# Attention, SoLU block and GELU-like block: the bias table from one position row with scalars, one layer-norm step deferred, products three chunks behind

## The chip, the cores and the metric

The kernel runs on one core of a Trainium2 chip. The metric is the time that the device needs for one execution, in microseconds (us). The engines are TensorE (PE in the profile; PEld is its weight load), VectorE (DVE), ScalarE (ACT), GpSimd (POOL) and SyncE (SP, which here only issues DMAs). Less is better.

## The reference

Three parts follow one another: attention with a position bias, a SoLU block with a layer norm, and a block with a piecewise quadratic activation. All is in float32.

```
scores = q @ k.T / sqrt(64)                     # 4 batches, 8 heads, 576 positions, 64 per head
x[i,j] = log1p(|i-j|) / log1p(max(i,1))
bias   = relu(x * w1 + b1) @ w2                 # 32 hidden values -> one bias for each head, i, j
attn   = softmax(scores + bias);  y = attn @ v  # y as 2304 rows of 512

h  = y @ w_in                                   # 512 -> 1024
s  = h * softmax(h)
ln = (s - mean(s)) / sqrt(var(s) + 1e-6) * g
z  = ln @ w_out                                 # 1024 -> 512

h2 = z @ w_in2                                  # 512 -> 2048
g2 = h2 if h2 >= 1; 0 if h2 <= -1; else (h2+1)^2/4
out = g2 @ w_out2                               # 2048 -> 512
```

In row i, x[i,j] depends on j only by log1p(|i-j|). Row 1 has log1p(distance) divided by log1p(1), which is log 2; every row i > 1 is row 1 times the reciprocal of its own entry at distance i.

## The kernel before

**Bias stage.** The table of all biases is written to DRAM (`bias_d`) before the attention starts, by 36 units of 16 rows i each. A unit u covers `span(u)` distances, between 304 and 576 (`n`, mean 440). A loaded constant holds x for all rows as a high and a low part (`xcon`, 18 loads, one for two units). `emit_z` (L226) spreads it: for each of four quarters c TensorE multiplies the rows (`xs`) by a selection table that holds w1 (`sel`), so that partition 32a + h holds x times w1[h] for one row; the results lie in PSUM as `z` (L235, and L240 for the columns past 512). `relu` (L220) adds b1 and takes the positive part, on ScalarE (L222) for the first pair of quarters and for the rest past 512, on VectorE (L224) for the second pair. `emit_c` (L245) multiplies these 128 x n tiles `r` by w2 on TensorE (L254), one quarter for each 32 output partitions, into `o`; ScalarE and VectorE copy `o` mirrored (L260) and straight (L264) to `ow`, and SyncE stores it (L269). The order on every engine is the order in which the code emits: `emit_z` of unit p, then `emit_c` of unit p - 1. `ow` has six buffers, `r` three. In between, `prep_all` (L172) prepares the first heads in steps of its generator: it casts q and k on VectorE to high parts (L181, L184) and subtracts on GpSimd for the low parts (L183, L186); one step is taken in every second unit. Loads of the stored table (`load_bias`) are issued after units 12, 17, 27, 33 and at the end, on SyncE's queue between the stores.

**Attention.** 144 chunks k (16 units of two heads, nine chunks each) run in an order that strings of letters write out: Q scores (L394) and their sum with the bias tile (L400), E exponential, T transposition, P product with v, B a step of `prep_all`, W a step of a conversion of the weights. B is left out in the first unit.

**SoLU and layer norm.** For each of 18 tiles of 128 rows: `emit_h` (L535), then `emit_post` (L541) as a generator: maximum (L553), exponential, product and sum (L558), square (L563), the inverse root on GpSimd (L568), and the last step: a multiplication of two columns on VectorE (L570) and the normalisation on ScalarE (L571). `emit_lt` transposes the tile two iterations later (L677, L681, L685), `emit_o` (L696) multiplies by w_out, and ScalarE copies the result out (L701). Steps of the conversion of the next weights (`bw`, L291 to L310 and L281) stand in between.

**Last block.** 80 chunks (j, f): `emit_h2` (L820) into `h`, then the activation to `ga` (L826 to L828), its high part `gh` on ScalarE (L829) and low part `gl` on VectorE (L831); `emit_o2` (L844) multiplies the chunk of two steps before by w_out2 and sums over f. `gh` and `gl` have three buffers.

## Time and profile before

| | us |
|---|---|
| median of three runs | 988.68 (986.91 to 991.41) |
| profiled execution | 988.0 |
| its span | 986.2 |
| TensorE busy | 966.6 (98%) |
| VectorE busy | 616.2 (62%) |
| ScalarE busy | 548.6 (56%) |
| GpSimd busy | 311.4 (32%) |

The span runs from the first to the last instruction of the profile; the profiled execution's own time lies 1.8 us above it. Matmuls are pipelined and their ends are modelled, so a busy TensorE is not one at its peak, but a gap in its row is real waiting. The granted TensorE clock is a share of full speed.

### The profile page before, as it was taken

Reading aid. Unit: us, or ns where it says so; the run is one execution under the profiler, and the core shown is the slowest. Engines: PE = TensorE matmul, PEld = TensorE weight load, DVE = VectorE, ACT = ScalarE, POOL = GpSimd, SP = SyncE. Lnnn points to the kernel's source line nnn. Section 1 sums busy time; section 2 is a strip of 40 time slices with the busy share of each in tenths; the row PEclk is TensorE's granted clock in tenths of the full one; section 3 lists DMA queues with packets and bytes.
Section 4 is the critical chain, followed back from the end, with each engine's and each line's share of the span. In section 5 each row is a group of like instructions: output and inputs, shape, how many; then the busy total and the mean of one; then the engine's idle time right before and its main releaser. Section 6 shows DMA issues by size and latency. Waiting matters only on the chain.

```text
span 986.2 us, 16218 instructions
## 1 busy us (share of the span) xinstructions
PE 966.6 (98%) x6112; PEld 798.4 (81%) x6112; DVE 616.2 (62%) x1232; ACT 548.6 (56%) x1116; POOL 311.4 (32%) x277
## 2 busy tenths in 40 slices
PE   9999999999999999999999899989999999999998
PEld 6447888888888878899998888768888888888897
DVE  6778878779779536777777747774434343433343
ACT  6888888889889856666666433332222222222232
POOL 3323455555555312555555423430010011000000
PEclk9999999999999999999999999999999999999999
DMA  6995474463562100234544468501000100100010
GB/s 188 281 302 166 140 235 138 137 221 127 175 198 100 36 15 8 86 129 150 171 160 160 160 241 304 200 14 64 12 11 1 64 21 1 53 7 6 1 43 22
DMA packets 50046, 112.21 MB, mean 114 GB/s; under 512 B 7600, under 2 KB 13872, under 8 KB 49968
## 3 DMA queue, kind: packets, MB, share of 16 engines
q1 hardware_dynamic: 42688, 101.72, 31.4%
q0 software_dynamic: 2384, 4.74, 1.8%
q10 hardware_dynamic: 4896, 4.72, 1.4%
q8 instruction: 48, 0.79, 0.3%
q14 instruction: 30, 0.25, 0.1%
HBM read 80.34 MB, written 30.82 MB: 113 GB/s over the span
## 4 chain that ended last, share of the span: by engine, by line
PE 40%; issue 8%; POOL 6%; DVE 5%; ACT 2%; DMA 0%; POOLq 0%; ACTq 0%; DVEq 0%
PE acc L844 17%; PE h L820 17%; PE ps_x L696 3%; PE ps_s L535 2%; POOL wp L304 2%; POOL wdl L281 2%; DVE ga L827 1%; POOL xl L519 1%; DVE wp L291 1%; DVE raw L294 1%; POOL stb L568 1%; DVE ga L828 1%; PE ps_s L696 1%; DVE wp L295 1%; ACT gh L829 1%
## 5 line engine op out<-in xcount | busy, mean ns | idle before, releaser
L827 DVE SCALAR_TENSOR_TENSOR ga<-ga 128x512 f32<-128x512 f32 (+1 forms) x80 | 56.8, 710 | 157.5 <-ACT ga L826 157.5
L826 ACT ACTIVATE ga<-h,half_c 128x512 f32<-128x512 f32 (+1 forms) x80 | 51.5, 644 | 131.1 <-PE h L820 131.1
L400 DVE CUSTOM_DVE_ANT_0 e<-ps_s,bt 128x576 f32<-128x576 f32 x144 | 106.6, 752 | 25.3 <-PE ps_s L394 22.2
L820 PE MATMUL h<-x2h,w2l 128*128 128x512 f32 (+1 forms) x320 | 117.7, 368 | 0.0
L820 PE MATMUL h<-x2l,w2h 128*128 128x512 f32 (+1 forms) x320 | 117.7, 368 | 0.0
L820 PE MATMUL h<-x2h,w2h 128*128 128x512 f32 (+1 forms) x320 | 117.6, 368 | 0.0
L415 ACT ACTIVATE e<-e,su 128x576 f32<-128x576 f32 x144 | 112.3, 781 | 6.5 <-DVE su L400 6.2
L844 PE MATMUL acc<-w2h,gh 128*128 128x512 f32 x288 | 112.7, 391 | 2.5 <-ACT gh L829 2.5
L304 POOL TENSOR_TENSOR wp<-raw,wp 128x256 f32<-128x256 f32 (+1 forms) x64 | 68.3, 1067 | 148.1 <-DVE wp L301 115.3
L844 PE MATMUL acc<-w2h,gl 128*128 128x512 f32 x288 | 112.5, 391 | 1.5 <-DVE gl L831 1.5
L829 ACT CAST gh<-ga 128x512 fp32r<-128x512 f32 (+1 forms) x80 | 46.2, 578 | 120.6 <-DVE ga L828 120.6
L844 PE MATMUL acc<-w2l,gh 128*128 128x512 f32 x288 | 112.3, 390 | 0.0
L733 POOL TENSOR_TENSOR x2l<-x2f,x2h 128x512 fp32r<-128x512 f32 (+1 forms) x20 | 25.6, 1281 | 253.2 <-ACT x2h L732 253.2
L394 PE MATMUL ps_s<-kh,sq 128*128 128x288 f32 x320 | 101.3, 334 | 3.7 <-DVE su L400 3.5
L458 ACT COPY pt<-ps_t 128x512 f32<-128x512 f32 x144 | 83.6, 581 | 24.1 <-PE ps_t L457 23.7
L394 PE MATMUL ps_s<-kl,sq 128*128 128x288 f32 x320 | 89.0, 294 | 0.0
L457 PE MATMUL ps_t<-ident,e 128*128 128x128 f32 x576 | 86.8, 274 | 0.0
L831 DVE TENSOR_TENSOR gl<-ga,gh 128x512 fp32r<-128x512 f32 (+1 forms) x80 | 52.3, 653 | 48.3 <-ACT gh L829 48.1
L696 PE MATMUL ps_x<-lh,woh 128*128 128x256 f32 x256 | 73.5, 287 | 6.4 <-ACT os L701 5.5
L457 PEld LDWEIGHTS ps_t<-ident,e 128*128 128x128 f32 x576 | 69.6, 141 | 5.7 <-ACT pt L458 2.1
L696 PE MATMUL ps_x<-ll,woh 128*128 128x256 f32 x256 | 72.1, 282 | 0.5 <-DVE ll L685 0.5
L696 PE MATMUL ps_x<-lh,wol 128*128 128x256 f32 x256 | 72.1, 281 | 0.0
(147 smaller groups left out, 2277.9 us busy)
## 6 DMA issues: line engine op xcount, KB each, us to landing
stg<-in_qk_dram SPq DMA_DIRECT2D x30, 640.0 KB, 3.9
raw<-in_w2nd_dram SPq DMA_DIRECT2D x32, 512.0 KB, 3.7
bias_d<-ow SPq DMA_DIRECT2D x36, 295.5 KB, 4.1
w_d<-wdh SPq DMA_DIRECT2D x20, 256.0 KB, 2.9
w_d<-wdl SPq DMA_DIRECT2D x20, 256.0 KB, 2.5
w2h<-w_d SPq DMA_DIRECT2D x10, 512.0 KB, 5.9
w2l<-w_d SPq DMA_DIRECT2D x10, 512.0 KB, 6.4
v<-in_vp_dram SPq DMA_DIRECT2D x15, 320.0 KB, 3.9
```

What stands on the lines that cost most here:

```text
L304: nc.gpsimd.tensor_tensor(out=p, in0=t, in1=p, op=ALU.mult)
L394: nc.tensor.matmul(sc[:, hf, 0:HS], lhsT=l, rhs=r, start=j == 0, stop=j == len(parts) - 1)
L400: nc.vector.tensor_tensor_reduce(out=halves(e), in0=sc[:, :, 0:HS], in1=halves(b_t[hp, n]), scale=-1.0 / float(D) ** 0.5, scalar=3.0e38, o ...
L415: nc.scalar.activation(out=e, in_=e, func=ACTF.Exp, scale=-1.0, bias=su[:, n:n + 1], accum_out=su[:, 9 + n:10 + n])
L457: nc.tensor.transpose(tp[:, kt * 128:(kt + 1) * 128], e[:, c0:c0 + 128], ident)
L458: nc.scalar.copy(out=pt[:, 4 * h:4 * h + 4, 128 * o:128 * o + 128], in_=tp.rearrange("p (a b) -> p a b", a=4))
L696: nc.tensor.matmul(ob[:, a * 256:(a + 1) * 256], lhsT=l, rhs=r[:, f, :], start=f == 0 and j == 0, stop=f == K1 - 1 and j == 2,)
L820: nc.tensor.matmul(hp_, lhsT=l, rhs=r[:, kk, 0:n], start=kk == 0 and q == 0, stop=kk == KD - 1 and q == 2)
L827: nc.vector.scalar_tensor_tensor(out=a, in0=a, scalar=1.0, in1=a, op0=ALU.min, op1=ALU.mult)
L829: nc.scalar.copy(out=gh[:, 0:n], in_=a)
L831: nc.vector.tensor_tensor(out=gl[:, 0:n], in0=a, in1=gh[:, 0:n].bitcast(F32), op=ALU.subtract)
L844: nc.tensor.matmul(acc_t[j][q], lhsT=l, rhs=r, start=f == 0 and m == 0, stop=f == K2 - 1 and m == 2)
```

## The change

The bias stage no longer loads `xcon` and multiplies it by a selection table. Only the row of position 1 is loaded, its high and its low part as the two partitions of `x1`; two products with ones add the parts and spread the sum to all 128 partitions, and ScalarE copies it to `xr`. VectorE takes the reciprocals of its elements, four quarters of the partitions each with its own stride, and multiplies them by w1 (`dg`), which gives one scalar for each partition and quarter (`sc1`). A quarter of r is then one instruction from SBUF to SBUF: on ScalarE relu(scale * xr + b1), on VectorE max(scale * xr, -b1), in which b1 is left out and its product with w2 is added at the end (`kc`). ScalarE takes the first quarter in four of five units. The copies of `o` to `ow` are two per unit, both on ScalarE, with the constant as bias. Of `prep_all` eight steps run in the bias stage, with the subtractions of the first unit on VectorE, and the first attention unit takes steps too. In the layer norm, the multiplication of the last step moves from VectorE to ScalarE, and the step is taken in the next iteration, behind the maximum and exponential of the next tile. In the last block the second product follows three chunks behind (two in the first five), with four buffers of `gh` and `gl`.

```
-    def load_x(rb): ... nc.gpsimd.dma_start(out=t[:, 0:n], in_=xcon[:, rb, 0:n])
+    nc.scalar.dma_start(out=x1, in_=bass.AP(xcon.tensor, xcon.offset + XR, [[32 * XR, 2], [1, S]]))
...
     for _ in range(8):
+        nc.tensor.matmul(wz[:, 0:128], lhsT=wt, rhs=wt, start=True, stop=True)
...
+    for hf in range(2):
+        nc.tensor.matmul(
+            zx[:, hf, 0:HS], lhsT=one2, rhs=x1[:, hf * HS:hf * HS + HS], start=True, stop=True
+        )
+    for _ in range(12):
+        nc.tensor.matmul(wz[:, 0:128], lhsT=wt, rhs=wt, start=True, stop=True)
+    nc.scalar.copy(out=halves(xr), in_=zx[:, :, 0:HS])
...
+    for a in range(4):
+        ps_ = slice(32 * a, 32 * a + 32)
+        rows = xr.rearrange("p (t a) -> p t a", a=4)[ps_, (1 if a == 0 else 0):S // 4, a]
+        nc.vector.reciprocal(out=sc1[ps_, (1 if a == 0 else 0):S // 4], in_=rows)
+    nc.vector.tensor_scalar(out=sc1, in0=sc1, scalar1=dg[:, 32:33], scalar2=None, op0=ALU.mult)
+    for c in range(4):
+        nc.tensor.matmul(z[32 * c:32 * c + 32, 256:258], lhsT=flat(w2b),
+            rhs=kc[:, 4:6] if c == 0 else b1c.to_broadcast([128, 2]), start=True, stop=True)
+    nc.vector.tensor_copy(kc[:, 1:3], z[:, 256:258])
...
-            nc.gpsimd.tensor_tensor(out=kl, in0=ks, in1=kh.bitcast(F32), op=ALU.subtract)
+            eng = nc.vector if u == 0 else nc.gpsimd
+            eng.tensor_tensor(out=kl, in0=ks, in1=kh.bitcast(F32), op=ALU.subtract)
...
-    def emit_z(u): ...
+    def on_act(u):
+        return u % 5 != 4
+    def emit_r(u):
...
+        for c in range(4):
+            w = sc1[:, 4 * u + c:4 * u + c + 1]
+            if c == 0 and on_act(u):
+                nc.scalar.activation(out=r[:, c, 0:n], in_=xr[:, 0:n], func=ACTF.Relu, scale=w, bias=b1c)
+            else:
+                nc.vector.tensor_scalar(
+                    out=r[:, c, 0:n], in0=xr[:, 0:n], scalar1=w, scalar2=kc[:, 0:1], op0=ALU.mult, op1=ALU.max
+                )
...
+        o = ps0.tile([128, 2, 512], F32, tag="o", name="o", bufs=3)
...
-                nc.scalar.copy(out=ow[:, M - e:M - a], in_=o[:, a - lo:e - lo][:, ::-1])
-                copy = nc.scalar.copy if u % 2 else nc.vector.tensor_copy
-                copy(ow[:, M - 1 + a:M - 1 + e], o[:, a - lo:e - lo])
+        k0 = kc[:, 1:2] if on_act(u) else kc[:, 2:3]
+        nc.scalar.activation(out=ow[:, 0:M - 1], in_=o[:, 1:M][:, ::-1], func=ACTF.Identity, bias=k0)
+        nc.scalar.activation(out=ow[:, M - 1:M - 1 + F], in_=o[:, 0:F], func=ACTF.Identity, bias=k0)
...
-        if p % 2 == 0 and 2 <= p <= 32:
+        if p % 4 == 0 and 4 <= p <= 32:
             step(bg)
...
-        nc.vector.tensor_tensor(out=st[:, 4:5], in0=st[:, 4:5], in1=st[:, 6:7], op=ALU.mult)
-        nc.scalar.activation(out=sc, in_=sc, func=ACTF.Identity, scale=st[:, 6:7], bias=st[:, 4:5])
+        nc.scalar.activation(out=st[:, 7:8], in_=st[:, 4:5], func=ACTF.Identity, scale=st[:, 6:7])
+        nc.scalar.activation(out=sc, in_=sc, func=ACTF.Identity, scale=st[:, 6:7], bias=st[:, 7:8])
...
-            elif c == "B" and u > 0:
+            elif c == "B":
                 step(bg)
...
         step(bp)
+        drain(bl)
...
-        drain(bp)
+        bl = bp
...
+    drain(bl)
     drain(emit_lt(NTT - 2))
     step(bw, 4)
     emit_o(NTT // 2 - 2, 0)
-    step(bw, 4)
     drain(emit_lt(NTT - 1))
     step(bw, 4)
+    emit_o(NTT // 2 - 2, 1)
     drain(bw)
-    emit_o(NTT // 2 - 2, 1)
...
-        gh = wc.tile([128, 512], F32R, tag="gh", name="gh", bufs=3)
+        gh = wc.tile([128, 512], F32R, tag="gh", name="gh", bufs=4)
...
-    L2 = 2
+    L2, done = 3, 0
...
-        if s >= L2:
-            emit_o2(*seq[s - L2])
+        if done <= s - (2 if s < 5 else L2):
+            emit_o2(*seq[done])
+            done += 1
```

## Rows read from the trace of the kernel before

**Rows 1.** Stages: stretch, length, busy us (instructions) per engine, clock, DMA share, GB/s.
```profile
4.49:75.64 71.15, 70.88 (x531) 36.62 (x530) 51.96 (x67) 55.99 (x102) 20.68 (x25) 1.00 0.88 270
75.64:94.50 18.86, 16.99 (x125) 14.64 (x123) 15.73 (x40) 16.48 (x41) 5.16 (x5) 1.00 0.58 174
520.00:560.00 40.00, 35.01 (x249) 32.28 (x248) 28.37 (x51) 25.53 (x41) 18.52 (x16) 1.00 0.44 152
560.00:580.00 20.00, 18.58 (x155) 18.18 (x155) 12.73 (x17) 7.17 (x12) 10.80 (x8) 1.00 0.54 177
625.00:680.00 55.00, 51.50 (x220) 40.76 (x221) 35.62 (x45) 19.83 (x33) 17.22 (x12) 1.00 0.16 53
```

**Rows 2.** Order of time, TensorE, end of the bias stage: start, length, engine, line.
```profile
71.14 1.01 PE L254 MATMUL o<-r,w2b 128*32 128x480 f32 x8
72.08 1.19 PE L235 MATMUL z<-xs,sel 96*128 96x512 f32 x4
...
75.64 0.40 PE L394 MATMUL ps_s<-kh,sq 128*128 128x288 f32 x1
```

**Rows 3.** Order of time, TensorE, start of the kernel.
```profile
1.06 3.78 PE L132 MATMUL z<-wt 128*128 128x128 f32 x16 [1.06 <-DVE mhalf L134]
...
8.38 1.18 PE L254 MATMUL o<-r,w2b 128*32 128x512 f32 x16
```

**Rows 4.** VectorE: forms (busy us, mean ns), a line's shortest/median/longest ns, two neighbours.
```profile
L181 DVE CAST kh<-stg 128x576 fp32r<-128x576 f32 x16 | 7.3, 453 | 0.0
L224 DVE TENSOR_SCALAR r<-z,sml 128x1024 f32<-128x1024 f32 x10 | 12.8, 1283 | 6.7 <-PE z L235 6.6
L224 DVE TENSOR_SCALAR r<-z,sml 128x608 f32<-128x608 f32 x2 | 1.7, 847 | 0.3 <-PE z L235 0.3
L427 DVE RECIPROCAL su<-su 128x9 f32<-128x9 f32 x16 | 3.4, 214 | 0.6
L557 DVE RECIPROCAL stb<-stb 128x1 f32<-128x1 f32 x16 | 2.6, 164 | 0.5
...
L295 DVE TENSOR_SCALAR wp<-raw x64: 293/426/1549, 81.9 to 650.9; 128x256 uint32<-128x256 uint32 x32, 128x512 uint32<-128x512 uint32 x32
...
599.98 0.43 DVE L295 TENSOR_SCALAR wp<-raw 128x512 uint32<-128x512 uint32 x1
600.32 0.68 DVE L831 TENSOR_TENSOR gl<-ga,gh 128x512 fp32r<-128x512 f32 x1
```

**Rows 5.** ScalarE: forms with mean ns, and two neighbouring copies in order of time.
```profile
L222 ACT ACTIVATE r<-z,sml 128x1024 f32<-128x1024 f32 x10 | 11.1, 1115 | 5.2 <-PE z L235 5.1
L222 ACT ACTIVATE r<-z,sml 128x608 f32<-128x608 f32 x2 | 1.6, 775 | 0.2 <-PE z L235 0.2
L571 ACT ACTIVATE scb<-scb,stb 128x1024 f32<-128x1024 f32 x16 | 19.9, 1246 | 38.4 <-DVE stb L570 38.4
...
34.07 0.40 ACT L260 COPY ow<-o 128x287 f32<-128x287 f32 x1
34.36 0.42 ACT L264 COPY ow<-o 128x304 f32<-128x304 f32 x1
```

**Rows 6.** DMA: a stretch of the bias stage, and the issues of the stores.
```profile
40.00:60.00 20.00, 20.00 (x145) 9.64 (x144) 16.02 (x21) 16.75 (x30) 6.58 (x9) 1.00 0.99 313
...
bias_d<-ow SPq DMA_DIRECT2D x36, 295.5 KB, 4.1
```

**Rows 7.** Layer norm in order of time, and TensorE's waits of 500 to 600 us.
```profile
543.46 1.26 DVE L570 TENSOR_TENSOR stb<-stb 128x1 f32<-128x1 f32 x1 [0.44 <-POOL stb L568]
544.82 1.25 ACT L571 ACTIVATE scb<-scb,stb 128x1024 f32<-128x1024 f32 x1 [2.58 <-DVE stb L570]
546.48 0.58 ACT L701 COPY os<-ps_x 128x512 f32<-128x512 f32 x1
...
PE ps_x L696 <- ACT os L701: 5.0, 2, 3.2
```

**Rows 8.** TensorE's waits of 600 to 700 us: total, times, longest.
```profile
PE acc L844 <- ACT gh L829: 2.5, 3, 1.4
PE acc L844 <- DVE gl L831: 1.5, 2, 0.7
```

More of the change, by code (lines that the diff above doesn't have):

```diff
@@ L102, in tile_attention_moe_moe @@
     es_p0, ps0 = opened(pool("ps0", space=PS))
-    Wh = wa0.tile([96, 32], F32R, name="Wh")
-    sel = wa0.tile([96, 8, 4, 32], F32R, name="sel")
+    x1 = wa0.tile([2, S], F32, name="x1")
+    one2 = wa0.tile([2, 128], F32, name="one2")
+    xr = wa0.tile([128, S], F32, name="xr")
+    sc1 = wa0.tile([128, S // 4], F32, name="sc1")
+    dg = wa0.tile([128, 64], F32, name="dg")
     warm = wa0.tile([128, 32], F32, name="warm")
@@ L126, in tile_attention_moe_moe @@
     make_identity(nc, ident)
-    load_x(rbs[1])
-    load_x(rbs[2])
-    wz = ps0.tile([128, 2, 512], F32, tag="z", name="z", bufs=3)
+    wz = ps0.tile([128, 512], F32, name="wz")
     for _ in range(8):
-        nc.tensor.matmul(wz[:, 0, 0:128], lhsT=wt, rhs=wt, start=True, stop=True)
+        nc.tensor.matmul(wz[:, 0:128], lhsT=wt, rhs=wt, start=True, stop=True)
     nc.vector.memset(exp_c, -916.0 * 2.0**23)
     nc.vector.memset(mhalf, -0.5)
-    nc.vector.tensor_copy(Wh, W96)
-    nc.vector.tensor_copy(W96[0:64], Wh[0:64])
-    nc.vector.tensor_tensor(out=W96[64:96], in0=W96[64:96], in1=Wh[64:96], op=ALU.subtract)
-    for g, w in ((0, 2), (2, 2), (4, 4)):
-        nc.vector.tensor_tensor(
-            out=sel[:, g:g + w],
-            in0=sm[:, g:g + w].unsqueeze(3).to_broadcast([96, w, 4, 32]),
-            in1=W96.unsqueeze(1).unsqueeze(1).to_broadcast([96, w, 4, 32]),
-            op=ALU.mult,
-        )
+    nc.vector.memset(one2, 1.0)
+    nc.vector.memset(kc[:, 4:5], 0.0)
+    nc.vector.memset(sc1[:, 0:1], 1.0)
+    nc.vector.tensor_reduce(
+        out=dg[:, 0:32], in_=ident.rearrange("p (a h) -> p h a", a=4), axis=AX.X, op=ALU.max
+    )
+    z = ps0.tile([128, 512], F32, name="zs")
+    zx = ps0.tile([128, 2, 512], F32, tag="o", name="zx", bufs=3)
+    for hf in range(2):
+        nc.tensor.matmul(
+            zx[:, hf, 0:HS], lhsT=one2, rhs=x1[:, hf * HS:hf * HS + HS], start=True, stop=True
+        )
+    for _ in range(12):
+        nc.tensor.matmul(wz[:, 0:128], lhsT=wt, rhs=wt, start=True, stop=True)
+    nc.scalar.copy(out=halves(xr), in_=zx[:, :, 0:HS])
+    nc.vector.tensor_tensor(out=dg[:, 0:32], in0=dg[:, 0:32], in1=sml[:, 0:32], op=ALU.mult)
+    nc.vector.tensor_reduce(out=dg[:, 32:33], in_=dg[:, 0:32], axis=AX.X, op=ALU.add)
+    nc.vector.tensor_scalar(out=kc[:, 0:1], in0=b1c, scalar1=-1.0, scalar2=None, op0=ALU.mult)
+    nc.vector.tensor_copy(kc[:, 5:6], b1c)
     nc.vector.tensor_scalar(out=w2r, in0=w2r, scalar1=float(D) ** 0.5, scalar2=None, op0=ALU.mult)
@@ L152, in tile_attention_moe_moe @@
     )
+    for a in range(4):
[4 more added lines that the diff above has]
+    for c in range(4):
+        nc.tensor.matmul(
+            z[32 * c:32 * c + 32, 256:258],
+            lhsT=flat(w2b),
+            rhs=kc[:, 4:6] if c == 0 else b1c.to_broadcast([128, 2]),
+            start=True,
+            stop=True,
+        )
+    nc.vector.tensor_copy(kc[:, 1:3], z[:, 256:258])
     kh_t, kl_t, sq_t, v_t, stg_t = {}, {}, {}, {}, {}
@@ L218, in span @@
         return max(S - 16 * u, 16 * u + 16)
-    def relu(eng, r, z):
-        if eng == 0:
-            nc.scalar.activation(out=r, in_=z, func=ACTF.Relu, bias=b1c)
-        else:
-            nc.vector.tensor_scalar(out=r, in0=z, scalar1=b1c, scalar2=0.0, op0=ALU.add, op1=ALU.max)
-    def emit_z(u):
-        rb, n = u // 2, span(u)
+    def on_act(u):
+        return u % 5 != 4
+    def emit_r(u):
+        n = span(u)
         r = wa0.tile([128, 4, S], F32, tag="r", name="r", bufs=3)
         r_t[u] = r
-        lhs = [flat(sel[:, 4 * (u % 2) + c]) for c in range(4)]
-        m = min(n, 512)
-        for a in range(2):
-            z = ps0.tile([128, 2, 512], F32, tag="z", name="z", bufs=3)
-            for c in range(2):
-                nc.tensor.matmul(z[:, c, 0:m], lhsT=lhs[2 * a + c], rhs=xs_t[rb][:, 0:m], start=True, stop=True)
-            relu(a, r[:, 2 * a:2 * a + 2, 0:m], z[:, :, 0:m])
-        if n > 512:
-            z = ps0.tile([128, 2, 512], F32, tag="z", name="z", bufs=3)
-            for c in range(4):
-                nc.tensor.matmul(
-                    z[:, 0, 64 * c:64 * c + n - 512], lhsT=lhs[c], rhs=xs_t[rb][:, 512:n], start=True, stop=True
+        for c in range(4):
[5 more added lines that the diff above has]
+                    out=r[:, c, 0:n], in0=xr[:, 0:n], scalar1=w, scalar2=kc[:, 0:1], op0=ALU.mult, op1=ALU.max
                 )
-            relu(0, r[:, :, 512:n], z[:, 0, 0:256].rearrange("p (c j) -> p c j", c=4)[:, :, 0:n - 512])
     def emit_c(u):
@@ L740, in tile_attention_moe_moe @@
     drain(bp)
-    b2 = iter(())
+    b2 = bl = iter(())
     for i in range(2, NTT):
```

32 lines of the change are left out of this document (11 added, 21 removed).

## The prediction, made before the changed kernel ran

> **What bounds the kernel now.** I read first the busy time by stage, then the order of instructions inside the first stage, then the forms of the two vector engines, and last what TensorE waits for. The stage table [rows 1] shows TensorE busy for 70.88 of 71.15 us in the bias stage (4.49 to 75.64 us), 16.99 of 18.86 us in the first attention unit, 35.01 of 40 us and 18.58 of 20 us in two stretches of the layer norm, 51.50 of 55 us at the start of the last stage. Everywhere else it has no gap worth naming, so the time is TensorE's queue, and a change counts only where it takes work out of that queue or closes one of these gaps. In the bias stage each of the 36 units puts two things in the queue [rows 2]: the z products (L235, L240) and the o products (L254). At 71.14 us the o products of a unit start, at 72.08 us the next z products: 0.94 us for o at n = 480, and the z products that follow are issued over about as long. The first score product comes at 75.64 us, right behind the last o product. That start is what the change moves.
>
> **The bias stage.** The z products and their operand (18 xcon loads, the table sel) go. TensorE keeps only o: 0.94 us at n = 480, so about 36 x 0.94 x 440/480 = 31 us, 440 being the mean of n over the units. TensorE is therefore no longer the bound if its clock holds; what is late next is VectorE, ScalarE, or the bias stores.
>
> Start. Before, the first o product runs at 8.38 us [rows 3]. Now the eight warm products end at 4.84 us as before; behind them in TensorE's queue stand the two products that spread row x1. They have 576 columns, the eight warm ones 1024 in 3.78 us: 2.1 us at most, 1.1 us if the clock is up by then, I take 1.5. So the row is there at 6.3 us, and the copy to xr on ScalarE (576 elements, at most 0.75 us by the costs of [rows 5]) ends at 7.0 us. Then VectorE makes four reciprocals of 144 elements. The only rows for one are 214 ns at 9 elements and 164 ns at 1 [rows 4]: 6.1 ns for each element, so 0.16 + 143 x 0.0061 = 1.04 us, four of them 4.2 us. From below, at the rate of a cast, they take 0.9 us together. I take 4.2, as the rows are of this operation; with the multiplication of sc1 (0.25 us) the first r starts at 11.4 us and the first o product comes at about 13, near 5 us later than before. The twelve added warm products and the two-column products stand in TensorE's queue in this time and are hidden by the reciprocals; so are the small VectorE operations, done while x1 is on its way.
>
> The Trainium skill, "VectorE: DVE Perf Modes", section on the fixed hardware budget, says that a reciprocal is an iterative divide with a repeat count of 8; at the page's 0.96 GHz that would be an estimated 8.3 ns for each element and 5.4 us for the four. The row gives 6.1 ns, so measurement speaks for the smaller; by the page the start would be 1.2 us later.
>
> VectorE. r has four quarters in each unit; ScalarE takes one in 29 units, so VectorE has 29 x 3 + 7 x 4 = 115. A cast of 576 elements from SBUF takes 453 ns, and a two-operation tensor_scalar of 256 elements 293 ns at its shortest: 0.5 ns for each element and 153 ns fixed [rows 4]. Two scalars that are read from SBUF are not in those rows. The relu at L224 has one, and reads PSUM: 1283 ns at 1024 and 847 ns at 608, which is 1.05 ns an element and 210 ns fixed. So the fixed part lies between 153 and 153 + 2 x 60 = 273 ns; I take 210. A mean r operation is then 210 + 0.52 x 440 = 440 ns. Independent operations overlap by 0.09 us (L295 starts at 599.98 us and takes 0.43, L831 starts at 600.32) [rows 4], so one is paid with 0.35 us: 40 us in all, 34 to 47 between the ends. To this comes the preparation of unit 0, which now has its subtractions on VectorE: casts of 1.9 us, and four subtractions at 0.75 to 0.82 us (0.68 us at 512 elements), 5 us together. Sum 45 us, 39 to 52.
>
> ScalarE. A relu from PSUM costs 1115 ns at 1024 and 775 at 608: 0.82 ns an element and 278 ns fixed; with both scale and bias read from SBUF, 1246 ns at 1024, so 409 ns fixed [rows 5]. One r is 409 + 0.82 x 440 = 770 ns, 29 of them 22.3 us. All writing of ow is now on ScalarE: two copies a unit, 591 elements together, 2 x 278 + 0.82 x 591 = 1.04 us, 37.4 us for 36. Neighbours overlap by 0.11 us (34.07 us, 0.40 long, and the next at 34.36), some 10 us over 101 operations. Sum 49.7 us.
>
> So ScalarE is the longest by a little. With 2 us for waits on the o products it ends at 11.4 + 49.7 + 2 = 63.1 us, the last o product some 1 us before it, and with what the stores may add I set the first score product to 63.0 us: **12.6 us earlier**. Between the ends of VectorE's cost and of the reciprocals it lies at 58 to 66 us.
>
> Stores. 36 of 295.5 KB are 10.6 MB; with the remaining loads of this time (qk of four heads 2.6, v 0.3, bias tiles 2.0) 15.5 MB. At 0.99 of the DMA engines they move 313 GB/s [rows 6], so 50 us at the least, of which some 5 run before the first store. That fits the 52 us of the engines closely, without cover to spare.
>
> **First attention unit.** Eight of the 16 preparation steps in the bias stage go, and the first unit now gets them (the casts, two subtractions for each head on GpSimd). VectorE there is at 15.73 of 18.86 us and TensorE is not full [rows 1]. The casts add 1.9 us, partly in the part where VectorE and ScalarE are ahead of TensorE's queue. Bounds 0 and 3 us; I take **1.5 us later**.
>
> **Layer norm.** At 543.46 us a one-element VectorE multiplication takes 1.26 us, as long as the GpSimd operation beside it; ScalarE waits for it and runs the normalisation (L571) at 544.82 us, and only then, in its strict order, the copy of the output product (546.48 us), for which TensorE waits [rows 7]. The two waits of this kind are 5.0 us. The change puts the multiplication on ScalarE (about 0.2 us, not on TensorE's path) and the pair behind the maximum of the next tile, so ScalarE no longer stands before that copy; the transposition that needs it comes an iteration later. At the end of the phase the last transposition is no longer behind eight conversion steps; the 1.4 us that stand idle between 560 and 580 us [rows 1] may go too. Bounds 0 and 6.4; I take **5.0 us**.
>
> **Last stage.** Between 625 and 680 us TensorE stands for 3.5 us because gh or gl of the product two chunks back is late [rows 1, 8]: VectorE is held up by conversions. Three chunks is 3.6 us or so more room for the chain, after the first five. Behind 680 us no gap is left and none can go; at the end the same products are run in another order. Bounds 0 and 3.5; I take **3.0 us**.
>
> **Sum.** The profiled execution took 988.0 us (span 986.2), and 988.0 - 12.6 + 1.5 - 5.0 - 3.0 = 968.9 us. The median of the runs is 0.7 us above the profiled one: 969.5 us.
>
> **Rivals.**
> A: as above. With its own bounds 963 to 975 us. 0.62.
> B: TensorE's clock. The granted clock is 1.00 in every stretch of [rows 1], with the engine nearly always busy; the change leaves it idle for 2 to 3 us before the first o product and for about 0.5 us in every 1.4 us after. At the lower of its two levels, 1.2 instead of 2.4 GHz, the 31 us of o become 62, TensorE is the bound again, and the stage ends at 11.4 + 62 + 1 = 74 us, hardly earlier than before. For it speaks that nothing in the trace shows this pattern at full clock; against it, that a bound TensorE is busy again and that a granted 1.00 stands beside 35 busy of 40 us. Half of the stage at the lower level gives 979 us, all of it 981. 0.15. The Trainium skill, "TensorE: Matmul & The Clock Gate", section on the second failure mode of its clock monitor, says that an engine that idles briefly but often between groups swings between the two levels; no run here shows it yet.
> C: the stores bind. If they reach 270 GB/s, the mean of the bias stage [rows 1], and not 313, 14 MB from 14 us on last until 66, ScalarE waits for a free ow, and the score products start near 67 to 68 us: 974 us. 0.10.
> D, on the other side: the r operations run at one element per cycle, as the relu from PSUM does. Then one costs 210 + 1.05 x 440 = 670 ns, paid with 0.58, the 115 cost 67 us, VectorE 72, and the stage ends at 84 to 91 us instead of 75.6: 990 to 997 us, say 993.5. It decides from 0.56 us paid per operation on; at 0.35 we are far from it. Against it speaks the 293 ns row, which has two operations at the fast rate; for it, that no row has scalars read from memory at that rate. 0.06.
> E: the bias stage as in A, but the gaps of the layer norm and the last stage only move to another wait (the same conversions still hold VectorE and ScalarE): 977 us. 0.07.
>
> **Numbers.** The likeliest is 969.5 us. A, C and E and half of B lie in 961 to 982, and D and the unforeseen outside. Less than 0.5%, about 4.9 us, cannot be told from no change; all but D and part of what is unforeseen end below 983.7 us. So faster 0.92, the same 0.04, slower 0.04.
>
> **What would show it.** In the new profile: the first score product near 63 us; four reciprocals near 1 us each; the r operations on VectorE at 360 to 500 ns; the granted clock 1.00 in the bias stage; no wait of L696 for os; no wait of L844 after 625 us. It is wrong if the r operations take 600 ns and more, if the clock there is half, or if SyncE's stores are what ScalarE waits for.

## The result, and the profile after

The changed kernel takes 979.65 us (median), against 989.3 us for the kernel before on the same chip: a ratio of the means of 0.9893, interval 0.9848 to 0.9938. One of its four runs, 1045.19 us at a mean granted clock of 0.851 (0.996 in the others), is left out of the ratio; the other three have a median of 977.47 us. It is faster, by a little over half of what was forecast (969.5 us). The profiled execution took 977.47 us, span 975.7 us (before 988.0 and 986.2).

Here "span" is the time from the first to the last instruction of a profile. Both traces can be cut at the same products on TensorE: the first score product, the first product of the attention phase behind the first unit (L433 before, L443 after), the first transposition of the layer norm phase (L677, L687), its last output product (L696, L706), the end of the span. In us:

| stage | before | after | difference | predicted |
|---|---|---|---|---|
| bias stage, to the first score product | 75.64 | 65.84 | -9.8 | -12.6 |
| first attention unit | 21.79 | 26.28 | +4.5 | +1.5 |
| attention and middle | 275.59 | 275.94 | +0.3 | 0 |
| layer norm and output products | 209.67 | 202.84 | -6.8 | -5.0 |
| last stage | 403.53 | 404.81 | +1.3 | -3.0 |
| span | 986.2 | 975.7 | -10.5 | -19.1 |

The stage view of the kernel after (stretch, length, then busy us and instructions of TensorE, its weight loads, VectorE, ScalarE, GpSimd, then granted clock, DMA share, GB/s) answers to [rows 1]:

```profile
4.49:65.84 61.35, 46.23 (x391) 17.54 (x390) 57.95 (x130) 48.71 (x100) 0.58 (x1) 0.97 0.71 223
65.84:92.12 26.28, 21.86 (x149) 17.89 (x146) 21.05 (x51) 19.48 (x48) 13.85 (x12) 0.94 0.68 223
520.00:560.00 40.00, 39.98 (x294) 37.67 (x293) 28.25 (x49) 25.23 (x44) 20.66 (x17) 1.00 0.52 165
560.00:580.00 20.00, 19.05 (x129) 17.08 (x128) 8.95 (x13) 6.17 (x10) 6.70 (x5) 1.00 0.72 246
613.00:668.00 55.00, 51.08 (x219) 40.30 (x218) 39.18 (x50) 20.91 (x35) 16.80 (x12) 1.00 0.20 69
```

The reader is to see four things. TensorE has 15 us of gaps in the bias stage, and VectorE hardly one after its wait for the spread row (3.5 us); in the first attention unit VectorE is at 21.05 us (18.45 before) and GpSimd at 13.85 (8.01 before, in 21.79 us); the layer norm stretch that was busy for 35.01 of 40 us is full; in the last stage TensorE stands as long as before (51.08 busy of 55 us, before 51.50).

**The start and the bias stage.** The order of time (start, length, engine, line) answers to [rows 3]; the two rows under it group VectorE's operations by line (busy us, mean ns), the last two by shape:

```profile
4.77 1.54 PE L141 MATMUL zx<-x,one 2*128 2x288 f32 x4
6.35 0.64 ACT L146 COPY xr<-zx 128x576 f32<-128x576 f32 x1 [3.54 <-PE zx L141]
7.02 4.22 DVE L162 RECIPROCAL sc<-xr 32x143 f32<-32x143 f32 x4 [3.52 <-ACT xr L146]
...
11.61 2.52 DVE L255 TENSOR_SCALAR r<-xr,sc,kc 128x576 f32<-128x576 f32 x5
...
12.58 2.07 PE L268 MATMUL o<-r,w2b 128*32 128x512 f32 x7 [3.21 <-ACT r L253]
```

```profile
L255 DVE TENSOR_SCALAR r<-xr,sc,kc 128x576 f32<-128x576 f32 (+17 forms) x115 | 48.8, 507 | 0.1
L162 DVE RECIPROCAL sc<-xr 32x144 f32<-32x144 f32 (+1 forms) x4 | 4.2, 1044 | 3.6 <-ACT xr L146 3.5
...
L255 DVE TENSOR_SCALAR r<-xr,sc,kc 128x576 f32<-128x576 f32 x6 | 3.1, 578 | 0.0
L255 DVE TENSOR_SCALAR r<-xr,sc,kc 128x304 f32<-128x304 f32 x6 | 2.3, 438 | 0.0
```

The start came out as worked out: reciprocals of 1.04 us, first r at 11.61 us. An r operation is longer: (578 - 438) / 272 elements is 0.51 ns an element, so 281 ns are fixed. From there the stage lasts as long as VectorE works. Stretches of it and of the unit behind it, with TensorE's clock as the last figure but two:

```profile
13.00:15.50 2.50, 2.50 (x22) 1.78 (x20) 2.50 (x7) 0.38 (x2) 0.00 (x0) 0.50 0.00 0
...
20.00:40.00 20.00, 16.14 (x144) 5.24 (x136) 19.93 (x48) 18.20 (x39) 0.00 (x0) 1.00 0.72 201
40.00:60.00 20.00, 13.64 (x113) 3.39 (x112) 19.93 (x50) 18.74 (x41) 0.00 (x0) 1.00 0.91 294
70.00:74.00 4.00, 2.05 (x12) 1.56 (x12) 2.84 (x7) 1.74 (x4) 1.47 (x2) 0.96 0.93 300
74.00:77.00 3.00, 2.90 (x13) 2.76 (x13) 2.93 (x7) 2.67 (x7) 2.45 (x2) 0.50 0.66 207
```

VectorE is busy for 19.93 of 20 us, ScalarE for 18.20 and 18.74. TensorE's clock is 0.50, the lower of its two levels, in the stretch from 13 to 15.5 us, behind 3.2 us without a product, and from 74 to 77 us, behind 4 us with 2.05 us of products; in the kernel before it is 1.00 in every stage.

**The first attention unit**, in order of time (VectorE and GpSimd), and what SyncE's queue waited for (total, times, longest, up to 92 us):

```profile
70.92 0.76 DVE L410 CUSTOM_DVE_ANT_0 e<-ps_s,bt 128x576 f32<-128x576 f32 x1 [1.89 <-DMA bt<-bias_d]
...
75.09 1.72 DVE L305 SCALAR_TENSOR_TENSOR raw<-raw,wp 128x256 f32<-128x256 uint32 x1
...
81.16 0.46 DVE L202 CAST kh<-stg 128x576 fp32r<-128x576 f32 x1 [1.15 <-DMA stg<-in_qk_dram]
...
74.98 1.54 POOL L208 TENSOR_TENSOR sq<-stg,sq 64x640 fp32r<-64x640 f32 x1
...
SPq L231 <- DMA bias_d<-ow: 6.2, 3, 2.8
```

VectorE, in its strict order, waits 1.89 us for a bias tile whose load stands behind the stores, and 1.15 us for a cast's operand with the next score's addition behind it. With a third wait its waits for loads in the unit come to 3.3 us, against 1.2 in the kernel before. Beside GpSimd's subtraction at 74.98 us an operation takes 1.72 us; in the rebalanced kernel below the same one takes 0.43 without such a neighbour.

**Layer norm and last stage.** ScalarE at 542 us answers to [rows 7]; then TensorE's waits after 368 us:

```profile
542.01 0.28 ACT L580 ACTIVATE stb<-stb 128x1 f32<-128x1 f32 x1
542.32 1.24 ACT L581 ACTIVATE scb<-scb,stb 128x1024 f32<-128x1024 f32 x1
...
546.50 0.59 ACT L711 COPY os<-ps_x 128x512 f32<-128x512 f32 x1 [0.23 <-PE ps_x L706]
...
PE ps_x L706 <- ACT os L711: 1.3, 2, 1.0
...
PE h L831 <- DVE ga L839: 3.9, 4, 1.6
PE h L831 <- DMA w2l<-w_d: 0.9, 1, 0.9
```

The multiplication of 1.26 us is one of 0.28, the copy at 546.50 waits for nothing but its product, and TensorE's 6.9 us of waits in this phase (5.5 for os, 1.4 for the two parts of a transposed tile, lh and ll) are 1.3. In the last stage no wait of the second product is left (4.0 us in [rows 8]); the first product now waits as long, for an h buffer that VectorE (L839) has yet to read, and 0.9 us for a weight load.

### The profile page after: what moved, and what is told of

Its sections match the earlier page's. It is cut to its first block, busy times and chain, and to the rows that moved or that the text cites. A ratio compares the mean times of both kernels' runs of the same rounds, so it can differ in the third digit from the quotient of the medians.

```text
span 975.7 us, 15942 instructions
## 1 busy us (share of the span) xinstructions
PE 942.9 (97%) x5972; PEld 780.6 (80%) x5972; DVE 616.0 (63%) x1285; ACT 545.9 (56%) x1132; POOL 299.9 (31%) x255
## 4 chain that ended last, share of the span: by engine, by line
PE 74%; DVE 11%; issue 5%; POOL 4%; ACT 4%; DMA 2%; SPq 0%; POOLq 0%; DVEq 0%; ACTq 0%
PE acc L855 17%; PE h L831 17%; PE ps_s L545 8%; PE ps_s L404 7%; PE ps_x L496 6%; PE ps_x L706 5%; PE ps_t L467 5%; POOL wp L315 2%; DVE r L255 2%; PE ps_x L500 2%; DVE raw L305 2%; PE ps_t L443 1%; PE o L268 1%; POOL wdl L292 1%; DVE wp L302 1%
## 5 line engine op out<-in xcount | busy, mean ns | idle before, releaser
L315 POOL TENSOR_TENSOR wp<-raw,wp 128x256 f32<-128x256 f32 (+1 forms) x64 | 71.7, 1121 | 128.0 <-DVE wp L312 97.4
L706 PE MATMUL ps_x<-lh,woh 128*128 128x256 f32 x256 | 73.4, 287 | 1.3 <-ACT os L711 1.3
L205 POOL TENSOR_TENSOR kl<-stg,kh 128x576 fp32r<-128x576 f32 (+1 forms) x30 | 47.6, 1587 | 86.7 <-DVE kh L202 63.8
L831 PEld LDWEIGHTS h<-x2h,w2h 128*128 128x128 f32 x320 | 60.2, 188 | 17.1 <-DVE ga L839 6.4
```

The costliest lines, as they stand in the source:

```text
L315: nc.gpsimd.tensor_tensor(out=p, in0=t, in1=p, op=ALU.mult)
L706: nc.tensor.matmul(ob[:, a * 256:(a + 1) * 256], lhsT=l, rhs=r[:, f, :], start=f == 0 and j == 0, stop=f == K1 - 1 and j == 2,)
L831: nc.tensor.matmul(hp_, lhsT=l, rhs=r[:, kk, 0:n], start=kk == 0 and q == 0, stop=kk == KD - 1 and q == 2)
```

## The experiments

"Bias", "unit" and "last" are the stages of the table above, from each run's own profile. All ratios are to the kernel before. A stage comes from one profile a run; the last stage of the six profiles that have the changed kernel's code there lies between 403.85 and 405.15 us.

**Layer norm and lag, one at a time.** The lag is the number of chunks by which the second product follows the first. First the lag alone undone, then a fourth h buffer, then the layer norm edits undone.

```
-    L2, done = 3, 0            gh, gl bufs=4
+    L2, done = 2, 0            gh, gl bufs=3
```

> The last stage as before: second products two chunks behind, gh and gl with three buffers; the rest as changed. My theory: the lag of three gained nothing, since VectorE's conversions hold up the chain all the same and the wait has only moved from gh (the second product) to the h buffers in PSUM (the first product), and three instead of two second products stand behind the last first product. So the time is that of the changed kernel within 1.5 us, 978 to 981 us, the waits of the first product for L839's reader fall to under 1 us and the second product waits again for gh, 3 to 4 us in all; from the last first product to the last second one 4.0 us instead of 5.4. Rival, that the lag of three gave its 3 us and that something else took them: 3 us slower than the changed kernel, near 982.5.

Measured: 978.64 us, ratio 0.9894 (0.9868 to 0.992). The idle time before TensorE's products by line (last columns) shows the wait where it was before, 4.4 us of it, and the first product free:

```profile
L831 PE MATMUL h<-x2h,w2h 128*128 128x512 f32 (+1 forms) x320 | 117.9, 368 | 0.1
L855 PE MATMUL acc<-w2h,gh 128*128 128x512 f32 x288 | 112.8, 392 | 2.9 <-ACT gh L840 2.9
L855 PE MATMUL acc<-w2h,gl 128*128 128x512 f32 x288 | 112.8, 392 | 1.5 <-DVE gl L842 1.5
```

The last stage is 406.02 us, 1.2 longer than with the lag: up to the last first product it loses 2.6 us (397.62 against 395.04), behind it it gains 1.4 (8.40 against 9.76). The 1.2 us net are of the size of the spread; the two parts are clear of it. Of the 2.6, 1.4 us are no gain: with the lag one second product more stands behind the last first product. My "no gain" was a little too low and the rival's 3 us far too high; that the wait only moved is shown (4.4 us here, 3.9 in the changed kernel).

```
-        hp_ = ps2.tile(..., tag="h", name="h2", bufs=3)     acc bufs=5
+        hp_ = ps2.tile(..., tag="h", name="h2", bufs=4)     acc bufs=4
```

> The changed kernel with four instead of three PSUM buffers for h and four instead of five for the accumulators of the second products. My theory: with three chunks of lag the first product waits because all three h buffers are still to be read by VectorE; a fourth takes 2.5 to 3.5 us of these 3.9 us of waiting away, and the span falls to 972 to 973.5 us. Rival 1, VectorE's conversions hold the chain longer than any buffer can cover: the waits move back to the second product (gh), span 975 to 976. Rival 2, the missing accumulator makes TensorE wait for the output at the boundary between two token blocks: span 976 to 978, with waits of the second product on the reader of acc.

Measured: 976.44 us, ratio 0.9863 (0.9841 to 0.9885), span 973.1. No wait for an h buffer or an accumulator is left, but the second product waits again:

```profile
L855 PE MATMUL acc<-w2h,gh 128*128 128x512 f32 x288 | 112.6, 391 | 0.8 <-ACT gh L840 0.8
L855 PE MATMUL acc<-w2h,gl 128*128 128x512 f32 x288 | 112.5, 391 | 1.4 <-DVE gl L842 1.4
```

2.2 us of 3.9 remain, and the last stage is 403.25 us, 1.6 better (the span's other gain is a shorter unit, 24.69 us, less a start 0.7 us later). The five profiles with four h buffers, this one and those at the end of the section, have 402.58 to 403.38 us there, all below the six with three. So rival 1 has more of it than my theory: a buffer covers a part, and the waits follow VectorE's chain to whichever product comes next.

```
-        nc.scalar.activation(out=st[:, 7:8], in_=st[:, 4:5], ..., scale=st[:, 6:7])
+        nc.vector.tensor_tensor(out=st[:, 4:5], in0=st[:, 4:5], in1=st[:, 6:7], op=ALU.mult)
-        bl = bp
+        drain(bp)
```
(and the order at the end of the phase as before)

> The layer norm as before (multiplication on VectorE, normalisation in the same iteration, last transposition behind the conversions), the rest as changed. My theory: the whole gain between the first output product of that phase and its last (6.8 us by comparing the two traces) is this edit; the last output product of the layer norm phase comes 6 to 7 us later than in the changed kernel, at 577 to 578 us, TensorE waits for os for some 5 us again, and the span is 982 to 983 us. Rival, that part of it came from the earlier stages and the filler steps only falling otherwise: under 3 us lost, span under 979.

Measured: 982.18 us, ratio 0.9925 (0.9899 to 0.9951), span 981.6. The phase takes 209.38 us against 202.84: its whole gain is this edit. But the last stage is 402.45 us, 2.4 better than with the edit. Its first 10 us, without the edit and then in the changed kernel:

```profile
579.13:589.13 10.00, 10.00 (x47) 8.30 (x46) 4.82 (x8) 3.04 (x5) 0.00 (x0) 1.00 1.02 380
```

```profile
570.90:580.90 10.00, 9.05 (x41) 6.93 (x40) 3.14 (x5) 2.56 (x5) 0.92 (x1) 1.00 0.97 345
...
DVE wp L302 <- DMA raw<-in_w2nd_dram: 2.3, 1, 2.3
```

With the edit the phase ends sooner, the loads for the last stage do not: SyncE, behind its stores of converted weights, issues the first raw weights 2.4 us after the last output product starts (573.27 against 570.90 us), without the edit 1.7 us before it (577.46 against 579.13). TensorE waits 0.9 us for w2l and VectorE 2.3 us for the first raw weights, and the conversions start that much later. The last stage has thus been measured in all four combinations: 403.53 (neither edit), 402.45 (lag alone), 406.02 (layer norm alone), 404.81 (both). By these four single profiles the lag is worth 1.1 to 1.2 us and the layer norm edit costs the last stage 2.4 to 2.5; with the spread of 1.3 us, each is known to about 1 us.

**The preparation of the heads.**

```
-        if p % 4 == 0 and 4 <= p <= 32:
+        if p % 2 == 0 and 2 <= p <= 32:
-            elif c == "B":
+            elif c == "B" and u > 0:
```

> The preparation as before: 16 steps in the bias stage, none in the first attention unit; the rest as changed. My theory: the first unit lost 4.8 us (from the first score product to the first product of the second phase) partly for the preparation's casts, which stand in VectorE's strict order before the bias additions and wait for loads; without them the first unit is 2 to 3 us shorter, and the bias stage, bound by VectorE, 1.5 to 2 us longer (eight casts' work of 1.9 us, less what its gaps take): span 974.5 to 976, no gain that can be measured. Rival, that the first unit is bound by the late bias tile and by TensorE's lower clock alone: the first unit keeps its loss, and the bias stage's 2 us come on top, span 977 to 978.

Measured: 980.18 us, ratio 0.9908 (0.9881 to 0.9934), bias 72.91, unit 23.19. The unit is 3.1 us shorter, the bias stage 7.1 longer, far more than the casts. Beside each of GpSimd's four subtractions one r operation lasts 1.55 to 1.71 us and ends some 0.2 us behind the subtraction; the others keep their length. So the seven of 128x400 have a mean of 651 ns (479 in the changed kernel). The second line gives the shortest, median and longest of eight r operations around the subtraction of the third:

```profile
L255 DVE TENSOR_SCALAR r<-xr,sc,kc 128x400 f32<-128x400 f32 x7 | 4.2, 651 | 0.0
...
L255 DVE TENSOR_SCALAR r<-xr,sc,kc x8: 459/474/1704, 46.6 to 51.0; 128x400 f32<-128x400 f32 x3, 128x368 f32<-128x368 f32 x3, 128x416 f32<-128x416 f32 x2
...
48.03 1.66 POOL L208 TENSOR_TENSOR sq<-stg,sq 64x640 fp32r<-64x640 f32 x1 [2.33 <-DVE sq L206]
```

The same with these four subtractions on VectorE:

```
-            eng = nc.vector if u == 0 else nc.gpsimd
+            eng = nc.vector if u <= 1 else nc.gpsimd
```

> As the kernel with the preparation as before (16 steps in the bias stage), and the four subtractions of the second pair of heads are on VectorE instead of GpSimd; the rest as changed, with the four reciprocals and three h buffers. My theory: in the kernel with the preparation as before GpSimd's four subtractions cost VectorE 4.7 us (r operations of 128x352 to 128x416 took 610 to 690 ns beside them instead of 458 to 490), so on VectorE, at 0.75 to 0.82 us each, 3.1 us, they cost 1.5 us less: first score product at 71.3 us instead of 72.9. Rival, that the longer r operations have another cause (stores and loads at 0.97 of the DMA engines): they stay as long, the subtractions come on top, first score product at 75 to 76 us.

Measured: 976.82 us, ratio 0.9871 (0.9848 to 0.9894), bias 70.44, unit 22.52.

```profile
L255 DVE TENSOR_SCALAR r<-xr,sc,kc 128x400 f32<-128x400 f32 x7 | 3.0, 481 | 0.0
```

The r operations are back at 481 ns, so GpSimd was the cause. About 1 us of the 2.5 is an earlier start (first o product at 12.27 against 13.32 us); from there the stage lasts 58.2 us against 59.6. The Trainium skill, "SBUF — State Buffer", section "SBUF: two separate sides", says that GpSimd and some VectorE operations take one port pair in turn, the later one waiting for the whole of the other's instruction. The trace agrees: one r operation ends 0.2 us behind each subtraction, at a cost to VectorE of 1.1 to 1.2 us (for 128x400, 7 x 172 ns).

**The order of the bias tiles.**

```
-    rbs = [0, 17, 1, 16, 2, 8, 3, 9, 4, 10, 5, 11, 6, 12, 7, 13, 14, 15]   27: (4, 5), 33: (2, 3)
+    rbs = [0, 17, 1, 16, 2, 4, 3, 5, 6, 8, 7, 9, 10, 12, 11, 13, 14, 15]   27: (2, 3), 33: (4, 5)
```

> The units of the bias table in another order, so that the tiles of rows 128 to 255, which the first attention unit reads second, are stored and loaded before those of rows 256 to 383; the rest as changed. My theory: the first unit's VectorE waits 1.9 us and TensorE 2.3 us near 71 us because that tile's load is issued only at 65.4 us, behind a wait for the last stores, into full DMA engines; with the order changed this wait goes, the lower clock from 74 to 77 us may go with it (1.3 us), and the first unit is 1.5 to 3.5 us shorter: span 972 to 974. Rival, that whichever tile is late the full DMA engines delay the first unit: the wait moves to the next tile, span 975 to 976.5.

Measured: 976.26 us, ratio 0.988 (0.9857 to 0.9902), bias 65.70, unit 24.28, span 972.6. The unit is 2.0 us shorter than in the changed kernel's profile. But it is 24.27 and 24.69 us in the first two experiments too, and 26.76 us in the third, whose code is the changed kernel's up to there. So the unit varies by some 2.5 us from execution to execution, and this run doesn't tell the order of the tiles from chance.

The profiles show what the unit varies with: VectorE's waits for loads in it (bias tiles, operands of casts, raw weights). In us:

| | unit | VectorE's waits for loads | the rest | clock in the unit |
|---|---|---|---|---|
| changed kernel | 26.28 | 3.3 | 23.0 | 0.94 |
| lag undone | 24.27 | 1.4 | 22.9 | 1.00 |
| four h buffers | 24.69 | 2.0 | 22.7 | 1.00 |
| layer norm as before | 26.76 | 4.1 | 22.6 | 1.00 |
| tile order | 24.28 | 1.6 | 22.7 | 1.00 |
| one scalar (below) | 26.52 | 4.1 | 22.5 | 1.00 |
| 36 warm products (below) | 24.68 | 1.8 | 22.9 | 1.00 |
| kernel before | 21.79 | 1.2 | 20.6 | 1.00 |
| preparation as before | 23.19 | 2.1 | 21.1 | 1.00 |
| the same, subtractions on VectorE | 22.52 | 1.7 | 20.8 | 1.00 |

In the first seven, whose unit has the same code but for the order of the tiles, the rest is 22.5 to 23.0 us, and the two longest of these units have their clock at 1.00 throughout. So the waits, not the clock, carry the difference. The waits of the longest one (layer norm as before), by what ended them (total, times, longest):

```profile
DVE e L410 <- DMA bt<-bias_d: 1.5, 3, 1.0
DVE kh L202 <- DMA stg<-in_qk_dram: 1.4, 1, 1.4
DVE wp L302 <- DMA raw<-in_win_dram: 1.2, 1, 1.2
```

That is a sum over profiles; no run made the loads come early.

**The price of a scalar read from memory.**

```
-  out=r[:, c, 0:n], in0=xr[:, 0:n], scalar1=w, scalar2=kc[:, 0:1], op0=ALU.mult, op1=ALU.max
+  out=r[:, c, 0:n], in0=xr[:, 0:n], scalar1=w, scalar2=0.0, op0=ALU.mult, op1=ALU.max
```

> The second scalar of VectorE's r operations is the constant 0.0 instead of a column read from SBUF (this leaves the clamp at -b1 out); the rest as changed. My theory: these operations cost 0.52 us per 1000 elements x 1000 and 278 ns fixed, of which each scalar read from memory is about 60 ns; with one fewer they are 50 to 70 ns shorter (128x576: 510 to 530 instead of 578), and as VectorE bounds the bias stage the first score product comes 115 x 0.06 = 5 to 7 us earlier, at 59 to 61 us, if ScalarE (91% busy) or the stores do not bind first; with ScalarE as the next bound 62 to 63. Rival, that the fixed part does not depend on where the scalars come from: same length of the operations, first score product at 65.8 us.

Measured: 975.86 us, ratio 0.9864 (0.9849 to 0.9879), bias 63.68, unit 26.52. VectorE's forms, and a stretch of the stage:

```profile
L255 DVE TENSOR_SCALAR r<-xr,sc 128x576 f32<-128x576 f32 x6 | 2.8, 516 | 0.0
L255 DVE TENSOR_SCALAR r<-xr,sc 128x304 f32<-128x304 f32 x6 | 1.9, 370 | 0.0
...
30.00:50.00 20.00, 12.33 (x128) 2.67 (x120) 18.32 (x52) 19.21 (x43) 0.00 (x0) 1.00 0.92 296
```

An operation is 62 to 68 ns shorter, 207 ns fixed instead of 281. Now ScalarE binds (19.21 of 20 us), and the stage ends at 63.68 us, 0.7 us behind the end of my expectation that has ScalarE as the next bound (62 to 63). This is near where the prediction had put it, with an r operation at 210 ns fixed and ScalarE as the bound (63.0). The run leaves the clamp at -b1 out: it prices the scalar and is no version to keep.

**TensorE's clock in the bias stage.**

```
-    for _ in range(12):      # warm products behind the spread
+    for _ in range(36):
```

> 36 instead of 12 warm products behind the spread of x1, so that TensorE is not idle while the reciprocals run; the rest as changed. My theory: the granted clock, which shows 0.50 from 13 to 15.5 us, is then 1.00 from the first o product on, but the first score product comes at 65.8 us all the same (within 0.4), since VectorE bounds the stage. Rival, that the clock costs at the start of the stage: 0.8 to 1.5 us earlier.

Measured: 979.88 us, ratio 0.9913 (0.989 to 0.9937), bias 69.61: neither. The added products run until 13.9 us, and behind them in TensorE's queue stand the two-column products whose result VectorE copies ahead of r:

```profile
5.67 8.31 PE L145 MATMUL wz<-wt 128*128 128x128 f32 x72
...
13.90 0.19 PE L166 MATMUL zs<-kc,w2b 128*32 128x2 f32 x1
...
14.21 0.16 DVE L173 COPY kc<-zs 128x2 f32<-128x2 f32 x1 [3.22 <-PE zs L166]
14.29 3.96 DVE L255 TENSOR_SCALAR r<-xr,sc,kc 128x576 f32<-128x576 f32 x8
```

r starts 2.7 us later than in the changed kernel: the cover of the reciprocals was used up. The other 1.1 us come in the stage: from VectorE's first r to the first score product it lasts 55.3 us, 54.2 in the changed kernel. The clock is now at its upper level at the start, but at 0.51 from 48.5 to 52 us, and there VectorE, which in the changed kernel never waits in the stage, waits for an o product to free a buffer of r:

```profile
48.50:52.00 3.50, 2.98 (x20) 0.55 (x24) 2.70 (x7) 3.11 (x8) 0.00 (x0) 0.51 1.00 324
...
50.38 1.26 DVE L255 TENSOR_SCALAR r<-xr,sc,kc 128x384 f32<-128x384 f32 x3 [0.80 <-PE o L268]
```

Two other runs have a stretch at the lower level in the middle of the stage too, at 43 to 46 us with the other tile order and at 47.5 to 50.5 us without the layer norm edits, but no such wait: from the first r the stage lasts 54.2 and 54.3 us. So a fall in the middle of the stage cost 0 to 1.1 us; at its start, in the changed kernel, VectorE waited for no o product.

**Towards a better version.** All with four h buffers. First one reciprocal for the four:

```
-        nc.vector.reciprocal(out=sc1[ps_, ...], in_=rows)                            # four times
+        nc.vector.tensor_copy(sc1[ps_].rearrange("p (f t) -> p f t", f=2), rows)     # four times
+    nc.vector.reciprocal(out=sc1, in_=sc1)
```

> The changed kernel with the four h buffers in PSUM, and one reciprocal of 128x144 elements instead of four of 32x144: four copies of 32x144 gather the elements from the spread row in PSUM first, beside ScalarE's copy of it; the twelve warm products stand behind the two-column products. My theory: the four reciprocals (4.2 us) stood on the path to the first r, and VectorE bounds the stage from there to its end: four copies take about 1 us and one reciprocal 1.05, so the first r starts at 8.6 to 9.0 us instead of 11.6, and the first score product comes 2 to 3 us earlier, at 63 to 64.5 us. Of that 1 to 2.5 us reach the end: span 970.5 to 972 (973.1 with the four h buffers alone). Rival, that the stores (DMA engines 96% busy from 40 us on) or ScalarE bind the end of the stage: first r at 8.8 us, first score product at 65 us or later, span 972.5 to 973.5.

Measured: 974.25 us, ratio 0.9842 (0.9815 to 0.9869), bias 65.66, unit 27.61, span 975.5.

```profile
7.76 1.27 DVE L159 COPY sc<-zx 32x144 f32<-32x144 f32 x4 [4.26 <-ACT xr L143]
...
9.18 1.05 DVE L161 RECIPROCAL sc<-sc 128x144 f32<-128x144 f32 x1
...
10.67 2.51 DVE L256 TENSOR_SCALAR r<-xr,sc,kc 128x576 f32<-128x576 f32 x5
```

The copies waited for ScalarE's copy from the same PSUM tile, and the spread itself took 2.28 us instead of 1.54; r starts at 10.67 us, 1.7 us earlier than in the first two experiments (12.35), which had the same spread, and the first score product comes 0.9 us earlier than theirs (66.56, 66.55). Missed by half: the copies waited, and in the middle of the stage, at the lower clock, VectorE waits 0.6 us for an o product. The unit took the rest back, VectorE waiting there 4.0 us for tiles, an operand and raw weights. The time is the rival's outcome, but in the profile VectorE, not ScalarE, works to the end of the stage.

Then the second pair's subtractions on VectorE as well (diff above):

> As the kernel with one reciprocal and four h buffers, and the four subtractions of the second pair of heads (in the first attention unit) are on VectorE instead of GpSimd. My theory: each of GpSimd's subtractions takes 1.6 us and lengthens VectorE's operations beside it by about 1.2 us in all, which is more than the 0.75 to 0.82 us that VectorE takes for the subtraction itself; so the first attention unit is 1 to 2 us shorter than in the kernel without this edit (24.3 to 24.7 us from the first score product to the first product of the next phase), and the span 1 to 2 us. Rival, that VectorE's own queue is what delays the scores: four subtractions of 0.8 us in it make the unit 1 to 3 us longer.

Measured: 974.55 us, ratio 0.9849 (0.9826 to 0.9871), bias 65.36, unit 26.75. The unit is 0.9 us shorter than in the run just above, but 2 us longer than in the first two experiments. Less VectorE's waits for loads (1.7 us) it is 25.1 us, against 23.6 in the run above (27.61 less 4.0) and 22.5 to 23.0 in the table; the two runs below, which keep this edit, have 25.0 each (26.33 less 1.3, 25.31 less 0.3), one of them with the clock at 1.00 throughout. VectorE is busy for 22.98 us of the unit, 21.96 in the run above. So by the profiles the rival holds, that the subtractions in VectorE's queue make the unit longer; the time shows no difference, and a rebalanced kernel without this edit was not run.

Then ScalarE takes its quarter of r in three units more:

```
-        return u % 5 != 4
+        return u % 9 != 8
```

> As the kernel with one reciprocal, four h buffers and the second pair's subtractions on VectorE, and ScalarE takes one quarter of r in 32 of the 36 units instead of 29. My theory: VectorE has three r operations fewer (1.5 us), ScalarE three more (2.3 us paid) on top of being 92 to 95% busy, so ScalarE binds and the first score product comes within 0.5 us of the kernel without this edit. Rival, that VectorE alone binds the stage: 1.5 us earlier.

Measured: 973.58 us, ratio 0.9839 (0.9814 to 0.9863), bias 64.35 (1.0 earlier, between the theories; 0.4 of it is a wait for an o product that the run above has at the lower clock), unit 26.33, span 971.6. Its ratio is the lowest of all, 0.5% below the changed kernel's (0.9839 against 0.9893), but the intervals overlap, and the four kernels of this part cannot be told apart by their times.

Last, the copies ahead of ScalarE's, half the warm products, and the other tile order:

> As the rebalanced kernel, with three more edits: VectorE's four copies of the spread row come before ScalarE's copy of it, six instead of twelve warm products, and the bias tiles of rows 128 to 255 are stored and loaded before those of rows 256 to 383. My theory: with the copies first the first r starts 0.6 to 1.0 us earlier and the first score product comes at 63.4 to 64.0 us (64.35 in the rebalanced kernel), the first attention unit takes 24.3 to 26 us instead of 26.3, since the tile that it reads second is there, and the span is 969.5 to 971.3. Rival, that neither is on the path: the stage ends with ScalarE's and VectorE's work, the unit with VectorE's queue, and the span is 971.6 within 0.4 unless TensorE's clock falls in the unit, which adds 1.5 to 2 us.

Measured: 973.57 us, ratio 0.9846 (0.9826 to 0.9866), bias 64.79, unit 25.31, span 971.5. r starts 0.7 us earlier than with the copies behind ScalarE's (10.01 us), the unit is 1.0 shorter, and the time is the same: the rival, within its 0.4. TensorE's clock was at its lower level for 10 us of the two stages in this profile, for none in the one above, and VectorE waits 0.6 us for an o product at 45 us; so what the edits are worth at equal clock stays open.

## Why the prediction was half right

The time lies inside the stated range, but outside A's own 963 to 975 us. That it falls on B's 979 is chance: what B priced did not happen.

- **Bias stage, start: right.** First r at 11.61 us (11.4 forecast), reciprocals 1.044 us (1.04).
- **Bias stage, VectorE: the term that was mis-sized.** "a mean r operation is then 210 + 0.52 x 440 = 440 ns ... paid with 0.35": it is 507 ns, paid with 48.8 / 115 = 0.42, so 8.6 us more in VectorE's queue. The slope was right; the fixed part is 281 ns, beyond the upper bound of 273, since two scalars are read from memory. VectorE and not ScalarE bounds the stage; with one of the scalars gone it ended 0.7 us behind where ScalarE was forecast. This is 2.8 us. The sum also had a small slip: 0.5 ns an element goes with 165 ns fixed in the two rows, not with 153.
- **First attention unit: 1.5 forecast, 4.5 measured.** The forecast counted the casts alone and put VectorE's waits for loads at nothing. They grew from 1.2 to 3.3 us in the changed kernel's profile, 2.1 of the 4.5, and between executions with this code they run from 1.4 to 4.1. The rest of the unit grew from 20.6 to 23.0 us, 2.4; with the preparation in the bias stage it is 20.8 and 21.1, so some 2 of the 2.4 are the preparation, with GpSimd's subtractions beside VectorE. What is left (0.2 to 0.5 us) was not traced. The lower clock is not needed for it: 26.76 us were measured at a clock of 1.00.
- **Layer norm: right, a little small.** 6.8 us, where 5.0 and the 1.4 named beside it make 6.4.
- **Last stage: wrong, 4.3 us and the largest miss.** The step that failed is "three chunks is 3.6 us or so more room for the chain": the room went to gh and gl alone, and the first product then waited for one of three h buffers. TensorE's waits were 4.0 us before, 3.6 with the lag alone and 3.9 with both edits (and 0.9 for a weight load), with a fourth h buffer 2.2. Up to the last first product the lag alone gave 2.75 us (395.45 before, 392.70 with the lag alone), which looks like the 3.0 forecast, but it came not from closed waits: "at the end the same products are run in another order" hid that three second products instead of two stand behind the last first product (8.09 us before, 9.75 with the lag alone), so 1.7 of the 2.75 only moved there. On top, the layer norm edit makes the last stage's loads late (2.4 us). That the wait went to the h buffers was rival E in part.
- **Rivals.** D fell (0.51 ns an element). C did not bind the stage (ScalarE waited for a store once, 0.6 us), but "without cover to spare" came true right behind it. B's clock did fall, but not for the stage, nor for half of it: between 40 and 60 us TensorE is busy for 13.64 of 20 us in short groups at a clock of 1.00. In the middle of the stage a fall cost 0 to 1.1 us, as TensorE is not what binds it. (B's 979 us for half of the stage also does not follow from its own numbers: 18 units at 1.72 us for o, against ScalarE's 1.38, add some 6 us to 969.5, near 976.) The Trainium skill, "TensorE: Matmul & The Clock Gate", section "A second HAM failure mode: psum-queue depth-cycling", says that an engine that idles often between groups swings between the two levels. The trace agrees in part: such falls come once or twice in most profiles of the bias stage and the unit, and in two, the preparation as before and the rebalanced kernel, not at all.

## What to carry to other kernels

When an edit takes the bound away from one engine, price the engine that is next by its exact form, scalars and all, and take the upper bound of an unknown that is multiplied by a hundred. A stage that ends earlier meets its successor's loads: ask for every gain which transfers of the next stage had been hidden by the time that goes. A longer lag in a loop needs buffers on both of its products, and part of it is paid back once at the loop's end.

## What the runs showed of the hardware

- A VectorE operation of the form multiply-and-maximum in fp32 has 281 ns fixed with two scalars read from SBUF, 207 with one, and 0.51 to 0.54 ns an element.
- A reciprocal takes 1.04 us for 143 or 144 elements, on 32 partitions as on 128.
- A GpSimd subtraction of 1.6 us beside VectorE's r operations holds one of them until 0.2 us behind its own end. It costs VectorE 1.1 to 1.2 us, more than the 0.75 to 0.82 us that VectorE takes to do it itself. In the attention unit, among other operations, the move to VectorE did not pay: the unit, less VectorE's waits for loads, was 25.0 to 25.1 us with it and 22.5 to 23.6 without.
